# Group 1's attention steps on a three-slot pitch with early key and query transposes, and weight splits ordered behind activations

## The chip, the cores and the metric

One core of a Trainium2 chip runs the kernel. The metric is the device time of one execution in microseconds (us); lower is better. Engines: PE is TensorE (matmuls and transposes), PEld its weight loads, DVE is VectorE, ACT is ScalarE, POOL is GpSimd, SP is SyncE, which here only issues DMAs.

## The reference

Inputs: q, k, v of 4 batches, 8 heads, 768 positions, 64 channels; two weight matrices, `w_in` 512 x 2048 and `w_out` 2048 x 512. All arithmetic is fp32.

```
scores = q @ k^T / 8, kept where key < n_sink (4) or 0 <= query - key < window (128)
a      = softmax(scores)                  (kept ones alone)
x      = (a @ v) with heads joined        -> 3072 tokens x 512
h      = x @ w_in
g      = h * erf(softplus(h))
out    = g @ w_out
```

## The kernel before, in words

The 3072 tokens are cut into 12 groups of 256 tokens, three to a batch. A group has an attention part and an MLP part.

**Attention** of a group is 4 steps, one per pair of heads; `s` counts steps over the whole kernel, so group 0 has steps 0 to 3, group 1 steps 4 to 7, group 2 steps 8 to 11. A step is a chain across engines:

- `prep` (L274): PE transposes two blocks of keys and two of queries into the PSUM tile `tqk`, and ACT copies it into the tile `kq` (L284), which has one place per head pair, used again by every group.
- `core`, `score` (L289, L298): PE forms the scores `ps` (L329), DVE swaps triangles (`copy_predicated`, L341), adds the mask and takes the row extremum (L346), ACT takes the exponential (L350).
- `norm` (L354): DVE forms the reciprocal of the sum (L357, L358), DVE or, for steps 4 to 7, ACT scales the rows (L365 or L363), DVE makes the sink part (L369).
- `ptrans` (L374): PE transposes the probabilities (`tp`, L381) and the sink part (`ts`, L382), ACT copies them out (L385, L390), POOL cuts triangles with four selects (L395).
- `av` (L400): PE multiplies by the values (L422); `xfin` (L428): ACT and DVE write the result as a high and a low part, `xh` and `xl` (L440, L441); group 0 has one fp32 tile, `xf` (L435).
- `kcopy` (L260) keeps the last key block for the next group, by an ACT copy in group 0 and by a DMA from SP later; `next_dup` (L246) refills the tile `vz` with group 1's values by three DMAs from SP.

`tqk`, `tp`, `ts` and `av` are tiles of one PSUM pool, `ps_t`, with two buffers (L141), taken in turn in the order of the program; the scores have a single buffer, `ps_s`.

**MLP** of a group is 16 positions `f`. `hidden` (L601) multiplies by a 128-column block of `w_in`, `act` (L614) works once per two positions on a 128 x 512 tile: ACT runs a tanh and five squares (L622, L623, L624, three times L627), DVE three products (L631). `project` (L640) multiplies by a block of `w_out` and accumulates. Two PSUM buffers hold `h`, each for a pair of positions; one comes free for the pair after next with the first product of its `act`.

Weights arrive as 32 blocks of 512 KB. `wconv` (L501) converts each with three DVE instructions (L511, L516, L519) into the plain block `wf`. Group 0 multiplies plain blocks alone (L606 and L649). Later hidden products (L610) and, from group 2, projections (L652 to L654) use blocks split in a high and a low part: `wsplit` (L523) rounds on ACT (L527) and subtracts on DVE (L528).

**Order.** Program time is cut into slots `a`; the MLP position `m` (16 g + f) is emitted in slot `m + 10`, its projection four slots later. `plan` (L452) says which stage of which step is emitted in which slot: `core` of a step in slot `pos(s)`, the others relative to it. Every emitted instruction has a priority, `256 * slot` plus an offset by kind (`O`, L45: attention -400 to -50, `act` -400, `wconv` 0, `ws` (split) 300, projection 900). A scheduler walks a simulated timeline and gives each engine, whenever it is free there, the most urgent instruction that is ready. The resulting order of each engine's queue is fixed, and on the chip every queue runs in that order. `follow` (L265) adds an order between two instructions of one engine, without a wait.

For steps 4 to 7 the slots before are 5, 9, 13 and 17 (`4 * s - 11`), their `prep` one slot ahead of that, their `av` two steps later, in `core(s + 2)`: slots 13, 17, 21 and 25. `wsplit` of block n is emitted in the slot of `m = 11 + n` for `w_in`, and of `m = 24 + 1.5 (n - 16)` for `w_out`.

Of the kernel before, what the change touches and what calls it, by code (L numbers as in the profile page):

```python
# [9 lines left out]
F32 = mybir.dt.float32  # L10
# [3 lines left out]
AF = mybir.ActivationFunctionType  # L14
ALU = mybir.AluOpType
# [14 lines left out]
CC = (-0.3597576685435788, 7.2931830957863735, 0.5777779046187317)  # L30
CK = 0.018644221205607978
CS = CK ** (1 / 6)
# [7 lines left out]
NE, AL = 4, 2  # L40
# [12 lines left out]
def kernel(  # L53
# [11 lines left out]
    nc = tc.nc  # L65
# [3 lines left out]
    NPAIR = H // 2  # L69
# [8 lines left out]
    scale = 1.0 / math.sqrt(D)  # L78
# [8 lines left out]
    b_a = [CS * a for a in CA]  # L87
# [43 lines left out]
    def fast_path():  # L131
        with ExitStack() as st:
# [19 lines left out]
                out=kw[:, :256], in0=rf[:, :256], scalar=0.0, in1=kw[:, :256], op0=ALU.is_ge, op1=ALU.mult  # L152
# [136 lines left out]
            def core(s):  # L289

                prev = None
                late = s - AL >= NE
                if late:
                    prev = av(s - AL)
                if s < NSTEP:
                    score(s, prev)
# [103 lines left out]
            def av(s):  # L400

                g, c = divmod(s, NPAIR)
                d = stp[s]
                gb = g % GPB
                a = d["av"] = ps_t.tile([P, GT], F32, tag="t", name=f"av_{s}")
                vt, pz = d["v"], d["pz"]
                pa = d["pa"].rearrange("p h i t -> p h (i t)")
                ops = []
                for j, (t0, t1) in enumerate(((0, HP), (HP, 3 * HP), (3 * HP, GT))):
                    if j > 0 or gb > 0:  # L410
                        x = vt[j] if isinstance(vt, list) else vt[:, j]
                        ops.append((x, pa[:, :, t0:t1], t0))
                for i in range(2):
                    for z, hf in enumerate((lo, hi)):
                        ops.append((vz[:, z, i, 2 * c : 2 * c + 2], pz[:, :, i, hf], P * i + HP * z))
                prev = None
                for m, (x, y, t0) in enumerate(ops):
                    for h in range(2):
                        o = a[64 * h : 64 * h + 64, t0 : t0 + y.shape[-1]]
                        prev = follow(  # L420
                            prev,
                            nc.tensor.matmul(  # L422
                                o, x[:, h, :], y[:, h, :], start=(m == 0), stop=(m == len(ops) - 1), skip_group_check=True
                            ),
                        )
                return prev
# [16 lines left out]
            def at(a, what):  # L443

                key = int(a * PW) + O[what] + (E.get(what, 0) if a < EA else 0)
                return tc.high_priority(offset=tc.tile_snap_priority() + 1 - key)

            def pos(s):

                return s if s < NE else 4 * s - 11  # L450

            plan = {}  # L452
            for s in range(NSTEP + AL):
                if s < NSTEP:
                    for what, fn, a in (
                        ("prep", prep, pos(s) - (3 if s < NE or s >= 2 * NPAIR else 1)), ("norm", norm, pos(s) + 1), ("ptrans", ptrans, pos(s) + 2),
                        ("load", load, pos(s) - 4),
                    ):
                        if what == "load":
                            if s < 2 * NPAIR:  # L460
                                continue
                            plan.setdefault(a, []).append(("load", load_v, s))
                        plan.setdefault(max(a, 0 if what == "prep" else -1), []).append((what, fn, s))
                    if s >= 2 * NPAIR:
                        plan.setdefault(pos(s) - 2, []).append(("dup", dup, s))
                    if s // NPAIR % GPB < GPB - 1:
                        plan.setdefault(pos(s) + (2 if s < NE else 1), []).append(("kcopy", kcopy, s))
                plan.setdefault(pos(s), []).append(("core", core, s))
                if s < NE:
                    plan.setdefault(pos(s) + 3, []).append(("av", av, s))  # L470
                    plan.setdefault(pos(s) + 4, []).append(("xfin", xfin, s))
                elif s - AL >= NE:
                    plan.setdefault(pos(s) + 1, []).append(("xfin", xfin, s - AL))
            STAGES = ("av", "xfin", "norm", "ptrans", "kcopy", "prep", "core", "dup", "load")

# [44 lines left out]
                    out=ti, in0=w[:, :, 0], scalar=29, in1=ti, op0=ALU.logical_shift_right, op1=ALU.bitwise_or  # L520
                )

            def wsplit(n):  # L523

                t = wf[n]
                d = wt[n] = wpool.tile([P, 2, DM], F32R, tag="wo", name=f"wt_{n}")
                nc.scalar.copy(d[:, 0, :], t)  # L527
                nc.vector.tensor_tensor(d[:, 1, :], t, d[:, 0, :].bitcast(F32), op=ALU.subtract)  # L528

            def wblock(n):  # L530
                if n < 16:
# [4 lines left out]
            mlp = make_mlp(work, ps_h, ps_o)  # L536
# [15 lines left out]
            for m in range(-LEAD, NG * NF + LAG + 2):  # L552
                a = m + LEAD
                live = 0 <= m < NG * NF
                if live:
                    g, f = divmod(m, NF)
                    if f % 2 == 0:
                        hp = mlp.hid_tile(m)
                    if f > 0:
                        with at(a, "hid"):  # L560
                            mlp.hidden(hp, xp[g], f)
                attn(a)
                w = m - LAG
                if 0 <= w < NG * NF:
                    g2, f2 = divmod(w, NF)
                    with at(a, "proj"):
                        mlp.project(gs[w // 2], g2, f2)
                    if f2 == NF - 1:
                        for i in range(2):
                            r0 = (g2 * 2 + i) * P  # L570
                            with at(a, "res"):
                                nc.sync.dma_start(out[r0 : r0 + P, :], mlp.result(g2, i))
                if live:
                    if f == 0:
                        with at(a, "hid"):
                            mlp.hidden(hp, xp[g], f)
                    if f % 2 == 1:
                        with at(a, "act"):
                            gs[m // 2] = mlp.act(hp, m, g < 2)

                while wn < 32 and a >= 1 and (wn < (0, 1, 3, 5)[a - 1] if a < 5 else wn < 2 * a - 4 or need(order[wn]) <= m + W1):
                    with at(a, "wc"):
                        wconv(order[wn], wn)
                    wn += 1
                    with at(a, "wl"):
                        for n in order[wl : wn + WQ]:
                            wload(n)
                            wl += 1
                for n in split.get(m, ()):
                    with at(a, "ws"):  # L590
                        wsplit(n)

    class make_mlp:
        def __init__(self, work, ps_h, ps_o):
            self.work, self.ps_h, self.ps_o = work, ps_h, ps_o
            self.acc = {}

        def hid_tile(self, m):
            return self.ps_h.tile([P, 2, GT], F32, tag="h", name=f"h_{m}")
# [14 lines left out]
        def act(self, hp, m, whole=False):  # L614
            work = self.work
            h = hp.rearrange("p a t -> p (a t)")
            r = work.tile([P, 512], F32, tag="r", bufs=1, name=f"r_{m}")
            if whole:
                acc = work.tile([P, 2, 512], F32, tag="g", bufs=2, name=f"gf_{m}")[:, 0, :]
            else:  # L620
                acc = None
            nc.scalar.activation(r, h, AF.Tanh, bias=b_t, scale=0.5)  # L622
            nc.scalar.activation(r, r, AF.Square, bias=b_v, scale=-0.5)  # L623
            nc.scalar.activation(r, r, AF.Square, bias=b_r)  # L624
            for i in range(3):
                u = work.tile([P, 512], F32, tag="u", bufs=UB, name=f"u{i}_{m}")
                nc.scalar.activation(u, r, AF.Square, bias=b_a[i], scale=CS)  # L627
                x = h if i == 0 else acc
                if acc is None:
                    acc = u  # L630
                nc.vector.scalar_tensor_tensor(out=acc, in0=u, scalar=CC[i] * CS**2, in1=x, op0=ALU.add, op1=ALU.mult)  # L631
            if whole:
                return (acc,)
            gt = work.tile([P, 2, 512], F32R, tag="g", bufs=2, name=f"g_{m}")
            gh, gl = gt[:, 0, :], gt[:, 1, :]
            nc.vector.tensor_copy(gh, acc)  # L636
            nc.gpsimd.tensor_tensor(gl, acc, gh.bitcast(F32), op=ALU.subtract)  # L637
            return gh, gl
# [168 lines left out]
```

## Time and profile before

| | |
|---|---|
| median of 3 runs | 775.43 us (774.27 to 777.92) |
| the profiled execution | 773.4 us |
| its span, first to last instruction | 771.6 us |
| mean granted TensorE clock | 0.978 of full speed |
| busy share of the span: PE, PEld, DVE, ACT, POOL | 94%, 78%, 64%, 71%, 26% |

The profile cuts the span in 40 slices of 19.3 us, so one can see at what time an engine was busy, not only how much on average. Each wait is put down to the instruction that released it. PE's busy time is modelled, since matmuls overlap; the start-to-start distance of a run of equal matmuls is the better measure of their cost.

### The profile page before, as it was taken

What the parts mean: (1) busy time and instruction counts of PE and PEld (TensorE: products, weight loads), DVE (VectorE), ACT (ScalarE), POOL (GpSimd) and SP (SyncE); (2) the same over time, 40 slices, a digit from 0 to 9 for tenths busy, and PEclk for the clock granted to TensorE, in tenths of its full rate; (3) what the DMA queues carried; (4) which work ended last, traced back from release to release, by engine and by line L of the source; (5) the groups of instructions that cost most, each with busy time, mean ns of one, the idle gap of its engine ahead of it and who ended that gap; (6) DMA issues with size and microseconds to landing.
All of it is one profiled execution on the core that took longest, in us unless ns stands there. A gap on an engine that the chain in (4) does not pass through costs nothing. (4 is left out here: it accounts for less than half of the span.)

```text
span 771.6 us, 16346 instructions
## 1 busy us (share of the span) xinstructions
PE 728.0 (94%) x5808; PEld 603.5 (78%) x5808; DVE 496.0 (64%) x1375; ACT 549.2 (71%) x1293; POOL 202.4 (26%) x281
## 2 busy tenths in 40 slices
PE   6689946999999999999999999999999999999997
PEld 3456624776788888888888888888888888888895
DVE  7999983566477476476476476476476476576352
ACT  4476855887597588588598587587597597597572
POOL 1220102201233332232242242242242242242221
PEclk9899969999999999999999999999999999999999
DMA  9999002211122122122222222212212212210000
GB/s 196 257 330 364 15 0 45 66 39 34 41 69 52 49 57 56 48 51 51 55 51 61 53 51 59 51 47 55 55 48 61 55 49 57 52 34 1 29 1 32
DMA packets 115112, 53.59 MB, mean 69 GB/s; under 512 B 93840, under 2 KB 107664, under 8 KB 115024
## 3 DMA queue, kind: packets, MB, share of 16 engines
q1 hardware_dynamic: 114192, 52.33, 25.8%
q8 instruction: 49, 0.80, 0.4%
q14 instruction: 39, 0.32, 0.1%
q10 hardware_dynamic: 832, 0.13, 0.1%
HBM read 38.54 MB, written 6.29 MB: 58 GB/s over the span
## 5 line engine op out<-in xcount | busy, mean ns | idle before, releaser
L610 PE MATMUL h<-xh,wt 128*128 128x256 f32 x1408 | 273.0, 284 | 10.3 <-DVE gf L631 7.3
L610 PEld LDWEIGHTS h<-xh,wt 128*128 128x128 f32 x1408 | 223.3, 188 | 19.0 <-DVE gf L631 7.2
L610 PE MATMUL h<-xl,wt 128*128 128x256 f32 x704 | 198.3, 283 | 0.0
L627 ACT ACTIVATE u<-r 128x512 f32<-128x512 f32 x288 | 161.5, 622 | 9.9 <-DVE gf L631 2.2
L637 POOL TENSOR_TENSOR g<-u,g 128x512 fp32r<-128x512 f32 x80 | 104.1, 1302 | 241.7 <-DVE g L636 216.7
L610 PEld LDWEIGHTS h<-xl,wt 128*128 128x128 f32 x704 | 132.3, 188 | 4.8 <-issue 1.0
L395 POOL TENSOR_SCALAR_AFFINE_SELECT pz<-pa 64x256 f32<-64x256 f32 x96 | 52.1, 543 | 313.2 <-ACT pa L385 310.0
L652 PE MATMUL o<-wt,g 128*128 128x512 f32 x320 | 129.5, 405 | 0.1
L631 DVE SCALAR_TENSOR_TENSOR u<-u,u 128x512 f32<-128x512 f32 x160 | 119.0, 744 | 15.9 <-ACT u L627 1.0
L653 PE MATMUL o<-wt,g 128*128 128x512 f32 x320 | 127.9, 400 | 0.0
L654 PE MATMUL o<-wt,g 128*128 128x512 f32 x320 | 124.5, 399 | 0.3 <-POOL g L637 0.2
L631 DVE SCALAR_TENSOR_TENSOR u<-u,h 128x512 f32<-128x512 f32 x80 | 54.9, 686 | 81.0 <-ACT u L627 75.5
L350 ACT ACTIVATE pst<-pst,neg 128x144 f32<-128x144 f32 x192 | 77.6, 406 | 15.1 <-DVE neg L346 13.2
L622 ACT ACTIVATE r<-h 128x512 f32<-128x512 f32 x96 | 57.0, 594 | 41.5 <-PE h L610 34.1
L654 PEld LDWEIGHTS o<-wt,g 128*128 128x128 f32 x320 | 59.0, 188 | 12.7 <-POOL g L637 0.6
L653 PEld LDWEIGHTS o<-wt,g 128*128 128x128 f32 x320 | 60.2, 188 | 11.0
L652 PEld LDWEIGHTS o<-wt,g 128*128 128x128 f32 x320 | 60.2, 188 | 10.7 <-issue 0.3
L649 PE MATMUL o<-wf,gf 128*128 128x512 f32 x128 | 60.2, 613 | 3.2 <-DVE gf L631 3.2
L624 ACT ACTIVATE r<-r 128x512 f32<-128x512 f32 x96 | 60.7, 633 | 2.7
L623 ACT ACTIVATE r<-r 128x512 f32<-128x512 f32 x96 | 61.0, 635 | 2.0
L636 DVE CAST g<-u 128x512 fp32r<-128x512 f32 x80 | 36.4, 455 | 36.1 <-PE o L654 32.8
L441 DVE TENSOR_TENSOR xl<-av,xh 128x256 fp32r<-128x256 f32 x44 | 18.5, 420 | 55.5 <-ACT xh L440 54.9
(85 smaller groups left out, 968.3 us busy)
## 6 DMA issues: line engine op xcount, KB each, us to landing
ws<-in_moe_w_in_dram SPq DMA_DIRECT2D x16, 512.0 KB, 6.7
ws<-in_moe_w_out_dram SPq DMA_DIRECT2D x16, 512.0 KB, 9.0
out_dram<-ot SPq DMA_DIRECT2D x24, 256.0 KB, 2.2
v<-in_v_dram SPq DMA_DIRECT2D x56, 96.0 KB, 2.4
q<-in_q_dram SPq DMA_DIRECT2D x80, 64.0 KB, 2.1
k<-in_k_dram SPq DMA_DIRECT2D x80, 64.0 KB, 2.1
vz<-v SPq DMA_DIRECT2D x80, 64.0 KB, 2.1
kq<-kq SPq DMA_DIRECT2D x28, 64.0 KB, 1.9
```

The costliest lines, as they stand in the source:

```text
L350: nc.scalar.activation(y, y, AF.Exp, bias=d["neg"][:, i, h : h + 1], scale=-1.0, accum_out=d["sum"][:, i, h : h + 1])
L610: nc.tensor.matmul(o, wt[NC * j + c][:, p, fs], xt[e][:, c, :], start=(m == 0), stop=(m == len(ops) - 1))
L622: nc.scalar.activation(r, h, AF.Tanh, bias=b_t, scale=0.5)
L623: nc.scalar.activation(r, r, AF.Square, bias=b_v, scale=-0.5)
L624: nc.scalar.activation(r, r, AF.Square, bias=b_r)
L627: nc.scalar.activation(u, r, AF.Square, bias=b_a[i], scale=CS)
L631: nc.vector.scalar_tensor_tensor(out=acc, in0=u, scalar=CC[i] * CS**2, in1=x, op0=ALU.add, op1=ALU.mult)
L637: nc.gpsimd.tensor_tensor(gl, acc, gh.bitcast(F32), op=ALU.subtract)
L649: nc.tensor.matmul(o, gt[0][:, ws], wf[16 + f], start=(f == 0), stop=(f == NF - 1))
L652: nc.tensor.matmul(o, gh[:, ws], wt[16 + f][:, 0, :], start=(f == 0), stop=False)
L653: nc.tensor.matmul(o, gh[:, ws], wt[16 + f][:, 1, :], start=False, stop=False)
L654: nc.tensor.matmul(o, gl[:, ws], wt[16 + f][:, 0, :], start=False, stop=(f == NF - 1))
```

## The change

Three things. `pos(s)` of steps 4 to 7 becomes `3 * s - 6` (slots 6, 9, 12, 15), with `prep` in slots 4, 4, 5 and 6, and `av` and `xfin` three and four slots behind the step's own `core`, as group 0 has them. `av` inside a later `core` begins with step 8. And each split's ACT and DVE instruction is given an order (`follow`) behind the last square and the last product of the `act` of an earlier pair: a split emitted at position m stands behind the pair of number `(m - 1) // 2 - 1`.

```diff
-                late = s - AL >= NE
+                late = s - AL >= 2 * NPAIR
...
-                return s if s < NE else 4 * s - 11
+                return s if s < NE else 3 * s - 6 if s < 2 * NPAIR else 4 * s - 11
...
-                        ("prep", prep, pos(s) - (3 if s < NE or s >= 2 * NPAIR else 1)), ("norm", norm, pos(s) + 1), ("ptrans", ptrans, pos(s) + 2),
+                        ("prep", prep, max(4, s - 1) if NE <= s < 2 * NPAIR else pos(s) - 3), ("norm", norm, pos(s) + 1), ("ptrans", ptrans, pos(s) + 2),
...
-                if s < NE:
+                if s < 2 * NPAIR:
                     plan.setdefault(pos(s) + 3, []).append(("av", av, s))
                     plan.setdefault(pos(s) + 4, []).append(("xfin", xfin, s))
-                elif s - AL >= NE:
+                elif s - AL >= 2 * NPAIR:
                     plan.setdefault(pos(s) + 1, []).append(("xfin", xfin, s - AL))
...
-            def wsplit(n):
+            def wsplit(n, m):
...
-                nc.scalar.copy(d[:, 0, :], t)
-                nc.vector.tensor_tensor(d[:, 1, :], t, d[:, 0, :].bitcast(F32), op=ALU.subtract)
+                x, y = mlp.mark[(m - 1) // 2 - 1]
+                follow(x, nc.scalar.copy(d[:, 0, :], t))
+                follow(y, nc.vector.tensor_tensor(d[:, 1, :], t, d[:, 0, :].bitcast(F32), op=ALU.subtract))
...
-                        wsplit(n)
+                        wsplit(n, m)
...
-                nc.scalar.activation(u, r, AF.Square, bias=b_a[i], scale=CS)
+                sq = nc.scalar.activation(u, r, AF.Square, bias=b_a[i], scale=CS)
...
-                nc.vector.scalar_tensor_tensor(out=acc, in0=u, scalar=CC[i] * CS**2, in1=x, op0=ALU.add, op1=ALU.mult)
+                pr = nc.vector.scalar_tensor_tensor(out=acc, in0=u, scalar=CC[i] * CS**2, in1=x, op0=ALU.add, op1=ALU.mult)
+            if isinstance(m, int):
+                self.mark[m // 2] = sq, pr
```

## Rows read from the trace of the kernel before

**Rows 1.** The page: busy tenths of the 40 slices (19.3 us each), and the granted clock of PE in tenths.
```profile
PE   6689946999999999999999999999999999999997
DVE  7999983566477476476476476476476476576352
PEclk9899969999999999999999999999999999999999
```

**Rows 2.** Busy time of each engine in stretches of 10 us. Columns: stretch, its length, busy us (and instructions) of PE, PEld, DVE, ACT, POOL, then PE's granted clock, DMA share, GB/s.
```profile
20.00:30.00 10.00, 4.64 (x34) 3.48 (x33) 9.70 (x39) 4.93 (x21) 1.87 (x4) 0.74 0.92 227
30.00:40.00 10.00, 7.44 (x81) 5.32 (x81) 9.53 (x18) 3.89 (x9) 4.95 (x8) 0.92 0.95 304
40.00:50.00 10.00, 7.63 (x51) 6.20 (x52) 9.91 (x29) 7.92 (x23) 0.00 (x0) 0.93 1.04 306
...
90.00:100.00 10.00, 7.37 (x34) 3.28 (x32) 10.00 (x19) 9.23 (x18) 0.00 (x0) 0.99 0.03 9
100.00:110.00 10.00, 2.13 (x5) 1.32 (x6) 9.91 (x18) 3.70 (x6) 0.00 (x0) 0.50 0.00 0
110.00:120.00 10.00, 9.44 (x25) 4.27 (x23) 2.87 (x14) 4.36 (x16) 0.00 (x0) 0.83 0.00 0
120.00:130.00 10.00, 6.61 (x88) 5.27 (x87) 4.51 (x16) 6.56 (x20) 3.48 (x7) 0.86 0.21 48
130.00:140.00 10.00, 6.76 (x78) 4.84 (x75) 5.55 (x21) 5.39 (x16) 2.56 (x6) 0.84 0.18 40
140.00:150.00 10.00, 9.38 (x105) 8.58 (x102) 6.39 (x23) 8.71 (x23) 2.06 (x4) 0.96 0.22 48
150.00:160.00 10.00, 10.00 (x55) 7.01 (x54) 7.21 (x23) 9.84 (x23) 0.00 (x0) 1.00 0.34 95
```

**Rows 3.** PE's timeline, 60 to 139 us: start, length, instruction, count, and in brackets the idle time before it and its releaser. L281 is `prep`, L329 the scores, L381 the transposes of the probabilities, L422 `av`.
```profile
60.81 0.99 PE L329 MATMUL ps<-kq 64*64 64x208 f32 x16
...
85.20 0.38 PE L281 MATMUL tqk<-ident,k_early 128*128 128x128 f32 x2
...
93.88 0.99 PE L329 MATMUL ps<-kq 64*64 64x208 f32 x16
...
104.68 0.58 PE L610 MATMUL h<-xh,wt 128*128 128x256 f32 x1 [6.38 <-DVE gf L631]
...
108.88 9.41 PE L649 MATMUL o<-wf,gf 128*128 128x512 f32 x16 [3.20 <-DVE gf L631]
...
119.40 0.44 PE L281 MATMUL tqk<-ident,k_early 128*128 128x128 f32 x2 [0.56 <-ACT pz L390]
...
121.17 0.99 PE L329 MATMUL ps<-kq 64*64 64x208 f32 x16
...
126.59 0.33 PE L381 MATMUL tp<-ident,pst 128*128 128x128 f32 x1 [3.15 <-ACT pst L363]
...
135.18 0.89 PE L381 MATMUL tp<-ident,pst 128*128 128x128 f32 x4 [2.62 <-DVE pst L365]
...
136.89 0.72 PE L422 MATMUL av<-pa,v_early 128*64 128x64 f32 x12 [0.62 <-ACT pa L385]
137.37 1.10 PE L422 MATMUL av<-pz,vz 128*64 128x64 f32 x16
```

**Rows 4.** ACT's timeline, 88 to 104 us, same columns; L527 is the split's rounding, L627 the last instructions of an `act`.
```profile
88.01 5.84 ACT L527 CAST wt<-wf 128x512 fp32r<-128x512 f32 x11
...
104.06 0.63 ACT L627 ACTIVATE u<-r 128x512 f32<-128x512 f32 x1
```

**Rows 5.** Groups of DVE's instructions from 88 to 112.3 us: line, operation, count | busy us, mean ns | idle before.
```profile
L528 DVE TENSOR_TENSOR wt<-wf,wt 128x512 fp32r<-128x512 f32 x21 | 13.5, 687 | 0.0
```

**Rows 6.** DVE's timeline, 96 to 126 us: the first product of positions 12 and 13 (it alone reads `h`), the first of step 6's four masks, the last product of group 0, then what a step costs DVE (here `xl` of step 5, and swaps and sink part of step 7).
```profile
96.86 0.70 DVE L631 SCALAR_TENSOR_TENSOR gf<-u,h 128x512 f32<-128x512 f32 x1
...
110.66 0.31 DVE L346 CUSTOM_DVE_ANT_0 pst<-ps,mask 128x144 f32<-128x144 f32 x1
...
111.58 0.69 DVE L631 SCALAR_TENSOR_TENSOR gf<-u,gf 128x512 f32<-128x512 f32 x1
...
122.20 0.41 DVE L441 TENSOR_TENSOR xl<-av,xh 128x256 fp32r<-128x256 f32 x1
122.64 0.90 DVE L341 COPY_PREDICATED ps<-tri,ps 64x256 f32<-64x256 int8 x2
...
126.08 0.29 DVE L369 TENSOR_TENSOR snk<-pst,sum 128x128 f32<-128x128 f32 x1
```

**Rows 7.** Groups of PE's instructions from 48 to 97 us, same columns as Rows 5.
```profile
L649 PE MATMUL o<-wf,gf 128*128 128x512 f32 x48 | 21.9, 594 | 0.0
```

**Rows 8.** POOL's timeline: the triangle selects of step 4 and of step 6, first pair of each.
```profile
54.73 3.73 POOL L395 TENSOR_SCALAR_AFFINE_SELECT pz<-pa 64x256 f32<-64x256 f32 x2 [14.86 <-ACT pa L385]
...
120.02 0.90 POOL L395 TENSOR_SCALAR_AFFINE_SELECT pz<-pa 64x256 f32<-64x256 f32 x2 [34.95 <-ACT pa L385]
```

**Rows 9.** DMA issues: line by tile, engine, count, KB each, median us from issue to landing.
```profile
vz<-v SPq DMA_DIRECT2D x80, 64.0 KB, 2.1
...
vz<-v_early SPq DMA_DIRECT2D x2, 128.0 KB, 10.2
```

**Rows 10.** SP's timeline of DMA issues: start, time from the first to the last of them, line, count. The last of the three `next_dup` issues, and the key copy of step 6.
```profile
53.76 0.46 SPq L250 DMA_DIRECT2D vz<-v_early  x1
...
94.56 0.50 SPq L129 DMA_DIRECT2D kq<-kq  x1
```

**Rows 11.** Waits of PE after 150 us: who waited for whom, total us, times, longest.
```profile
PE h L610 <- DVE u L631: 3.0, 8, 0.4
```

More of the change, by code (lines that the diff above doesn't have):

```diff
@@ L595, in __init__ @@
             self.work, self.ps_h, self.ps_o = work, ps_h, ps_o
-            self.acc = {}
+            self.acc, self.mark = {}, {}
         def hid_tile(self, m):
```

## The prediction, as it stood before the run

> **What bounds the kernel now.** I read the forty slices first, then stretches of 10 us where they dip, then the timelines of PE, ACT and DVE there. PE is at 9 tenths in nearly every slice from 140 us on [rows 1], so PE is the bound and a gain must be a hole in its line. There are two: the start, up to 50 us, and 90 to 150 us. In the second, PE is busy 7.37, 2.13, 9.44, 6.61, 6.76 and 9.38 of each 10 us [rows 2]: 41.7 of 60, so 18.3 us idle. From 150 us PE is full again, so what is closed there comes off the end.
>
> Two things make the hole. First, splits: ACT rounds eleven weight blocks from 88.0 to 93.9 us, and the `act` of positions 14 and 15 ends only with the square at 104.06 [rows 4]. DVE does 21 splits in 13.5 us between 88 and 112.3 [rows 5]; the first product of the pair before stands at 96.86, the last of group 0 at 111.58 [rows 6]. PE waits 6.38 and 3.20 us for such products [rows 3]. Secondly, attention: scores of steps 5, 6 and 7 come at 60.81, 93.88 and 121.17, the last two 8.7 and 1.8 us behind their own `prep` (85.20, 119.40), and the last `av` that group 1's hidden products need ends at 138.5; meanwhile PE waits 3.15 and 2.62 us for a step's scaled rows [rows 3]. A `prep` comes late because its PSUM tile is taken in turn behind `tp` and `ts` of the step before.
>
> **What may come back.** The idle time, 18.3 us. Then the clock: it is 0.50 in 100 to 110 us, where PE worked 2.13 us, and 0.83 to 0.96 until 150 [rows 2]. Group 0's last sixteen projections took 9.41 us [rows 3]; at the pace before they would take 16 x 21.9/48 = 7.3 [rows 7], so 2.1 us. For PE's other 22.8 busy us of 120 to 150, a clock near 0.85 against 1.00 bounds the loss at 22.8 x 0.15 = 3.4, and 0 bounds it below. I take 2.9, since the projections, the nearest row, did run slower in full: 5.0 in all (bounds 2.1 and 5.5). Together 23.3 us.
>
> **Does the work fit ahead of it?** DVE is full from 20 to 110 us [rows 1, 2], so its sum decides. A split at position m is ordered behind the `act` two or three positions earlier, which lets only six blocks (m = 11 to 16) go ahead of group 0's last `act`; 15 of the 21 leave, 15 x 13.5/21 = 9.6 us. What comes in is step 7 (swaps 0.90, four masks at 0.31, sink part 0.29, all shown, and about 0.3 for the reciprocal: 2.7 us) and three `xl` of 0.41: 3.9 us [rows 6]. Group 0's last product moves from 112.3 to about 106.6. PE: its projections end at 118.3; without the waits of 6.38 and 3.20 and the 2.1 us of clock, at 106.6. Three `av` (1.58 each, from 136.89 to 138.47), two sets of transposes (1.1), scores (0.99) and `prep` (0.88) of the steps moved ahead put back 8.8, at durations of the low clock [rows 3]: PE is done with all of it by 115, behind DVE. So PE can be full, and group 1's hidden products then need nothing more.
>
> **What the change costs.**
> - Four `prep` behind group 0's: three come earlier than before, as three more tiles in the turn of the two-buffer pool ahead of group 0's last `av`. Bounds: 4.3 us lost, three times a `prep` and the wait of 0.56 before one [rows 3]; 2.4 gained, if its products (0.8) only fill idle time. Between 20 and 50 us PE has 10.3 us idle and ACT more [rows 2], which covers them. I take 1.0 lost, nearer the cover.
> - 15 splits move behind 112 us, beside the 11 of the 32 that ran there. ACT has little room at first, 9.84 of 10 us at 150 [rows 2]. Queued behind a split on ACT stands the next square, for which DVE's product, then PE's hidden product wait. Bounds: 0, and 15 x 5.84/11 = 8.0 us [rows 4]. Those 11 and all later work left PE a wait of 3.0 us in all, at most 0.4 at a time [rows 11], so I take 2.0. The order itself adds no wait.
> - `av` of step 4 follows `next_dup` by one slot, not five. Its three DMAs were issued until 53.76 [rows 10] and took 10.2 us, where later ones take 2.1 [rows 9]: `vz` is there at 64. The first two of the step's four selects end at 58.5 [rows 8]. PE stops in its queue for 0 to 5.5 us, and everything behind it, hidden products included, waits. I take 1.0, since the rest of the selects and a queue of products stand between.
> - SP: key copies of steps 6 and 7 move from slots 14 and 18 to 13 and 16, and may stand ahead of the last weight loads, where step 6's copy came at 94.56 [rows 10]. A copy waits in SP's queue for its step's scores, the loads behind it too. The DMA share is down to 0.03 by 90 us [rows 2], so they have room; 0 to 5 us, I take 0.
> - POOL: the selects of the moved steps run beside a full DVE. A pair took 3.73 us at 54.73 and 0.90 at 120.02 [rows 8]: 2.8 us a pair, latency on a chain with three slots for a step. 0 to 3 us; I take 0.
> - Holes left by handing over between queues whose order was made on a simulated line: 0 to 6.4, the longest wait there [rows 3]; I take 1.5, as DVE's sum ends 8 us ahead of PE's.
>
> Sum: 23.3 - 1.0 - 2.0 - 1.0 - 1.5 = 17.8. The profiled execution, 773.4 us (span 771.6 and 1.8 around it), becomes 755.6; the median of the runs stands 2.0 higher, so **757.6 us**.
>
> The selects' rows show POOL losing beside a full DVE. The Trainium skill (SBUF — State Buffer, Who interferes with whom) says more: GpSimd and a DVE instruction with two SBUF inputs, or in a two-port mode, exclude each other through a shared port, and whichever issues first makes the other wait for its whole length. By that rule DVE may pay too, and the sum would go as in rival 3.
>
> **Rivals.**
> 1. *Steps keep their pace.* The late `prep` was not the brake; the hand-overs in DVE's full queue are. Step 6's scores came at 93.88 [rows 3], its first mask at 110.66 [rows 6]: 17 us of a pitch of 27 to 33. With 2 to 9 us saved a step (`prep` to scores), the last `av` ends some 10 us earlier, near 128, and the 23.3 become 10 less costs of 1 to 2: 767 for the runs. Against: scores of a step no longer stand behind transposes of the last, and three slots of priority replace four.
> 2. *Slower: splits in the way of `act`.* The place is `h`'s buffer: a hidden pair waits for the first product of the pair two before. If each of the 26 held-back splits comes ahead of that product, it adds 0.53 us of ACT and 0.64 of DVE [rows 4, 5]: 26 x 1.17 = 30.4, so 773.4 - 23.3 + 30.4 = 780.5, some 782.5 for the runs. It decides once ACT's queue for a pair is longer than PE's. For it: the 0.4 us waits at this very place [rows 11], and ACT's 9.84. Against: they are only 3.0 us in 620.
> 3. *POOL and DVE block each other.* Sixteen selects of 0.45 us, each holding DVE for its length, cost 7.2 us: group 0's last product at 113.8, its last eight projections (3.6 us) behind it at 117.4, and with hand-overs 4 to 5 us of the gain are lost: 762. Against: in the rows that show it, POOL waits, and nothing shows DVE waiting.
> 4. *Not what it says.* The slots are priorities alone. Step 5 was planned for slot 9 before too, ahead of the MLP's first position, and its scores ran at 60.81 [rows 3]. If the scheduler again places steps by readiness and moves the hole elsewhere, the time is 775.
>
> **How the numbers follow.** About 0.5% (3.9 us) is what a measurement of this kernel can tell from no change: 771.6 to 779.3. Forecast 0.60, rival 1 0.14, rival 3 0.06: faster 0.80. Rival 4: same 0.09. Rival 2: slower 0.11. The range: all of the clock, preps that fill idle time and no other cost give 18.3 + 5.5 + 2.4 = 26.2, so 749.2 for the runs; at the other end it takes in rivals 1 and 3 and stops at 770, below rivals 4 and 2, which are 0.20.
>
> **What would show it.** Right: PE has under 6 us idle between 90 and 150 us of the new profile and its clock stays near 1.00; group 0's sixteen last projections run at 0.46 us each; the last `av` of group 1 ends before 115 us; ACT has no run of splits ahead of an `act`; splits spread from about 90 to 220 us. Costs: PE's idle time in 20 to 50 us grows over 10.3 by no more than 1 or 2; PE's wait for L631 after 110 us stays under 5. Wrong: scores of steps 5 to 7 still 27 us or more apart (rival 1), L610 waiting over 20 us for L631 (rival 2), DVE instructions stretched beside L395 (rival 3), an idle stretch elsewhere as long as the old one (rival 4).

## The result and the profile after

The changed kernel takes 754.14 us (median of 4 runs, 753.5 to 756.13) against 776.67 in the same job: a ratio of 0.9716, 95% interval 0.9679 to 0.9752. Timed once more, in another job, it took 755.21 us, 0.9737 (0.9716 to 0.9759). The forecast was 757.6 us. The profiled execution has a span of 751.5 us, 20.1 less than before. Lines from 527 on are one to three higher than before: L527 is now L528, L606 L607, L610 L611, L624 L625, L631 L632, L649 L652.

The page after, the same lines as [rows 1]:

```profile
PE   6779899999999999999999999999999999999997
DVE  7999996665786665665665675576476476386342
PEclk9699999999999999999999999999999999999999
```

The dip of PE at 100 to 135 us is gone, and there is one digit of 8 where 9 stood, at 75 to 94 us. Stretches of the changed kernel, columns as in [rows 2]:

```profile
0.00:50.00 50.00, 33.98 (x281) 23.72 (x281) 43.46 (x162) 25.70 (x83) 10.79 (x25) 0.86 0.95 249
50.00:90.00 40.00, 35.40 (x216) 23.04 (x218) 39.03 (x96) 30.79 (x79) 18.11 (x12) 1.00 0.74 253
90.00:150.00 60.00, 59.81 (x390) 41.86 (x387) 44.35 (x109) 47.69 (x108) 7.62 (x15) 1.00 0.15 36
150.00:200.00 50.00, 48.30 (x398) 35.60 (x397) 31.32 (x96) 36.61 (x95) 9.10 (x16) 1.00 0.25 60
200.00:751.50 551.50, 542.78 (x4534) 475.39 (x4532) 336.96 (x918) 405.28 (x932) 166.40 (x215) 1.00 0.19 47
```

The same stretches of the kernel before:

```profile
0.00:50.00 50.00, 33.68 (x255) 22.59 (x256) 43.72 (x157) 26.12 (x84) 10.33 (x25) 0.92 0.96 247
50.00:90.00 40.00, 40.00 (x187) 27.57 (x187) 39.61 (x82) 28.19 (x58) 8.03 (x8) 0.97 0.69 249
90.00:150.00 60.00, 41.67 (x325) 27.56 (x324) 39.24 (x108) 37.94 (x98) 8.10 (x16) 0.83 0.11 24
150.00:200.00 50.00, 50.00 (x359) 35.05 (x360) 29.02 (x81) 38.36 (x89) 6.43 (x12) 1.00 0.18 44
200.00:771.60 571.60, 562.61 (x4695) 490.76 (x4686) 344.46 (x952) 418.56 (x967) 169.46 (x220) 1.00 0.20 48
```

Length less PE's busy time gives its idle time: 16.3, 0, 18.3, 0 and 9.0 us before, 16.0, 4.6, 0.2, 1.7 and 8.7 after. The hole of 18.3 us closed to 0.2; 4.6 opened at 50 to 90 us and 1.7 at 150 to 200. In sum 43.6 became 31.2, so 12.4 of the 20.1 us are idle time. The other 7.7 are PE's busy time, 728.0 to 720.3 for the same 5808 matmuls. The clock of 90 to 150 us rose from 0.83 to 1.00 and that of 50 to 90 from 0.97, while that of 0 to 50 fell from 0.92 to 0.86. These are the stretches from 48 us on in which the kernel before had a clock of 0.50, columns as above; the changed kernel stands at 1.00 in every stretch from 50 us on:

```profile
48.60:52.10 3.50, 3.50 (x10) 2.79 (x9) 3.50 (x8) 3.40 (x8) 0.00 (x0) 0.51 0.92 306
99.80:113.50 13.70, 5.63 (x9) 2.75 (x10) 12.98 (x31) 5.67 (x15) 0.00 (x0) 0.50 0.00 0
127.10:130.60 3.50, 3.29 (x39) 2.62 (x42) 0.03 (x1) 1.90 (x6) 1.67 (x4) 0.51 0.02 5
137.40:140.80 3.40, 3.40 (x42) 2.46 (x38) 2.39 (x5) 1.51 (x3) 1.51 (x3) 0.50 0.01 2
```

PE is busy for 15.8 us in them. Sixteen scores take 1.77 us there (at 138.40) and 0.99 at full clock (at 121.17), so, as an estimate, about half of the 15.8 was lost to the clock, near the 7.7. At the start the two kernels are even: PE is busy for 33.7 us of the first 50 before and for 34.0 after.

PE's timeline after, as [rows 3]:

```profile
42.34 0.44 PE L281 MATMUL tqk<-ident,k_early 128*128 128x128 f32 x2
...
42.93 0.99 PE L329 MATMUL ps<-kq 64*64 64x208 f32 x16
...
50.45 0.99 PE L329 MATMUL ps<-kq 64*64 64x208 f32 x16 [1.30 <-DVE neg L346]
...
56.48 0.34 PE L422 MATMUL av<-pa,v_early 128*64 128x64 f32 x4 [0.85 <-POOL pa L395]
57.23 0.55 PE L422 MATMUL av<-pa,v_early 128*64 128x128 f32 x8 [0.41 <-POOL pa L395]
...
61.45 0.99 PE L329 MATMUL ps<-kq 64*64 64x208 f32 x16
...
84.77 0.34 PE L422 MATMUL av<-pa,v_early 128*64 128x64 f32 x4 [1.94 <-POOL pa L395]
85.59 0.55 PE L422 MATMUL av<-pa,v_early 128*64 128x128 f32 x8 [0.48 <-POOL pa L395]
...
102.16 0.69 PE L422 MATMUL av<-pz,vz 128*64 128x64 f32 x16
...
103.26 3.60 PE L652 MATMUL o<-wf,gf 128*128 128x512 f32 x8
106.30 0.68 PE L611 MATMUL h<-xh,wt 128*128 128x256 f32 x1
...
115.73 3.70 PE L652 MATMUL o<-wf,gf 128*128 128x512 f32 x8
...
120.67 1.88 PE L652 MATMUL o<-wf,gf 128*128 128x512 f32 x4
```

All four transposes of group 1 are over by 43 us; scores of steps 5 to 7 come at 42.93, 50.45 and 61.45, where they came at 60.81, 93.88 and 121.17; the last `av` ends at 102.85, not 138.5, and group 1's hidden products begin at 106.30, ahead of group 0's last sixteen projections, which stand between 113.86 and 122.55. ACT's splits now stand in small lots between the squares, as in these lines of ACT's timeline (compare [rows 4]):

```profile
95.69 2.17 ACT L528 CAST wt<-wf 128x512 fp32r<-128x512 f32 x4
97.76 0.63 ACT L625 ACTIVATE r<-r 128x512 f32<-128x512 f32 x1
...
100.62 1.12 ACT L528 CAST wt<-wf 128x512 fp32r<-128x512 f32 x2
...
106.40 1.13 ACT L528 CAST wt<-wf 128x512 fp32r<-128x512 f32 x2
```

And POOL's selects of steps 4 to 6, with the first DVE lines behind the long one (POOL's timeline, then DVE's):

```profile
52.54 3.41 POOL L395 TENSOR_SCALAR_AFFINE_SELECT pz<-pa 64x256 f32<-64x256 f32 x2 [11.20 <-ACT pa L385]
...
63.66 2.59 POOL L395 TENSOR_SCALAR_AFFINE_SELECT pz<-pa 64x256 f32<-64x256 f32 x2 [6.49 <-ACT pa L385]
...
76.15 8.09 POOL L395 TENSOR_SCALAR_AFFINE_SELECT pz<-pa 64x256 f32<-64x256 f32 x2 [7.81 <-ACT pa L385]
84.30 1.23 POOL L395 TENSOR_SCALAR_AFFINE_SELECT pa<-pa 64x256 f32<-64x256 f32 x2
```

```profile
83.87 0.69 DVE L632 SCALAR_TENSOR_TENSOR gf<-u,h 128x512 f32<-128x512 f32 x1
84.46 0.80 DVE L519 SCALAR_TENSOR_TENSOR wf<-ws,wf 128x512 int32<-128x512 int32 x1
85.18 0.64 DVE L511 TENSOR_SCALAR wf<-ws 128x512 int32<-128x512 int32 x1
```

A pair of selects that takes 0.90 us where DVE is idle as it starts [rows 8] took 8.09. The pair ends as DVE works on a product that reads `h` from PSUM (83.87), and only then do DVE's next instructions stretch, 0.80 for 0.70 and 0.64 for 0.43.

### The profile page after: what moved, and what is told of

The parts are those of the page before. It is cut to its first block, busy times and chain, and to the rows that moved or that the text cites. A ratio compares the mean times of both kernels' runs of the same rounds, so it can differ in the third digit from the quotient of the medians.

```text
span 751.5 us, 16337 instructions
## 1 busy us (share of the span) xinstructions
PE 720.3 (96%) x5808; PEld 599.6 (80%) x5808; DVE 495.1 (66%) x1375; ACT 546.1 (73%) x1293; POOL 212.0 (28%) x281
## 5 line engine op out<-in xcount | busy, mean ns | idle before, releaser
L611 PE MATMUL h<-xh,wt 128*128 128x256 f32 x1408 | 271.4, 284 | 3.7 <-DVE u L632 3.5
L611 PEld LDWEIGHTS h<-xh,wt 128*128 128x128 f32 x1408 | 222.7, 188 | 12.9 <-DVE u L632 5.8
L611 PE MATMUL h<-xl,wt 128*128 128x256 f32 x704 | 199.0, 283 | 0.0
L395 POOL TENSOR_SCALAR_AFFINE_SELECT pz<-pa 64x256 f32<-64x256 f32 x96 | 61.4, 640 | 291.0 <-ACT pa L385 287.9
L611 PEld LDWEIGHTS h<-xl,wt 128*128 128x128 f32 x704 | 132.3, 188 | 5.2 <-issue 1.8
L632 DVE SCALAR_TENSOR_TENSOR u<-u,u 128x512 f32<-128x512 f32 x160 | 117.4, 734 | 15.5
L632 DVE SCALAR_TENSOR_TENSOR u<-u,h 128x512 f32<-128x512 f32 x80 | 54.8, 685 | 80.4 <-ACT u L628 79.9
L657 PEld LDWEIGHTS o<-wt,g 128*128 128x128 f32 x320 | 59.3, 188 | 12.4 <-POOLq L778 0.5
L625 ACT ACTIVATE r<-r 128x512 f32<-128x512 f32 x96 | 60.7, 632 | 2.8
L624 ACT ACTIVATE r<-r 128x512 f32<-128x512 f32 x96 | 60.9, 634 | 1.8
L652 PE MATMUL o<-wf,gf 128*128 128x512 f32 x128 | 59.0, 596 | 0.0
```

Of the source, the lines that this page charges most:

```text
L395: nc.gpsimd.affine_select(out=out, in_=x, pattern=[[0, 2], [0, 2], [-sg, HP]], compare_op=op, fill=0.0, base=0, channel_multiplier=sg,)
L611: nc.tensor.matmul(o, wt[NC * j + c][:, p, fs], xt[e][:, c, :], start=(m == 0), stop=(m == len(ops) - 1))
L632: pr = nc.vector.scalar_tensor_tensor(out=acc, in0=u, scalar=CC[i] * CS**2, in1=x, op0=ALU.add, op1=ALU.mult)
L652: nc.tensor.matmul(o, gt[0][:, ws], wf[16 + f], start=(f == 0), stop=(f == NF - 1))
L657: nc.tensor.matmul(o, gl[:, ws], wt[16 + f][:, 0, :], start=False, stop=(f == NF - 1))
```

## The experiments

My reading was that the two causes add up, and that within the second it is the late `prep` that holds a step back. Ratios are to the kernel before, timed in the same job, with 95% intervals.

**The two parts, each alone.** Steps moved, splits as before:

```diff
-                follow(x, nc.scalar.copy(d[:, 0, :], t))
-                follow(y, nc.vector.tensor_tensor(d[:, 1, :], t, d[:, 0, :].bitcast(F32), op=ALU.subtract))
+                nc.scalar.copy(d[:, 0, :], t)
+                nc.vector.tensor_tensor(d[:, 1, :], t, d[:, 0, :].bitcast(F32), op=ALU.subtract)
```

> The steps moved as in the change, splits without their order. Two causes in series (my reading): group 1's attention is done by about 105 us, but runs of splits again stand ahead of group 0's last activations, so PE waits some 6 to 9 us for L632 near 95 to 110 us; 760 to 765 us. Attention alone made the hole: 753 to 756 us. Splits alone made it: 772 to 777 us.

762.85 us, 0.983 (0.9779 to 0.9881). The last `av` ends at 109, but ACT rounds seven and six blocks in a row again, and PE waits for the products and for two selects. PE's waits from 84 to 130 us:

```profile
PE h L611 <- DVE gf L632: 3.9, 2, 2.1
PE av L422 <- POOL pa L395: 2.9, 2, 2.6
```

Splits ordered, steps as before (the change with `pos`, `prep`, `av` and `late` of the kernel before):

> Splits ordered as in the change, the steps as before. Two causes in series: group 0's projections end near 106 us, then PE idles while steps 6 and 7 still come 27 us apart; 765 to 772 us. Splits alone made the hole: 753 to 757 us. Attention alone made it: 774 to 777 us.

764.61 us, 0.9863 (0.9817 to 0.9909), 0.4 us under the range of my reading. Group 0's projections end at 108, but scores of steps 6 and 7 still come at 93.52 and 111.03 and the last `av` ends at 128. PE's longest waits from 90 to 140 us are the step's chain, as before, and one for a product:

```profile
PE tp L381 <- ACT pst L363: 2.7, 1, 2.7
PE tp L381 <- DVE pst L365: 2.6, 1, 2.6
PE o L652 <- DVE gf L632: 2.2, 1, 2.2
```

Against 774.66 in that job the parts alone win 11.8 and 10.1 us, 21.9 in sum; both together win 20.0 to 22.5 in their two jobs. So they add, and neither hides the other.

**What in the moved steps does it.** First the change with late transposes:

```diff
-                        ("prep", prep, max(4, s - 1) if NE <= s < 2 * NPAIR else pos(s) - 3), ("norm", norm, pos(s) + 1), ("ptrans", ptrans, pos(s) + 2),
+                        ("prep", prep, pos(s) - (3 if s < NE or s >= 2 * NPAIR else 1)), ("norm", norm, pos(s) + 1), ("ptrans", ptrans, pos(s) + 2),
```

> The change with the key and query transposes of steps 4 to 7 back one slot ahead of their step. If the late prep was the brake: scores of steps 5 to 7 fall back to 17 us or more apart (8 to 11 us in the changed kernel), the last av ends 10 us later or more, 757 to 764 us. If the slots alone matter: 753 to 756 us.

771.56 us, 0.9964 (0.9939 to 0.9989): worse than the range of my reading, and 7 us worse than not moving the steps at all. Scores come at 42.85, 70.02, 105.81 and 118.22. Then the reverse, early transposes with the old slots and the old, late `av`:

```diff
-                return s if s < NE else 3 * s - 6 if s < 2 * NPAIR else 4 * s - 11
+                return s if s < NE else 4 * s - 11
...
-                late = s - AL >= 2 * NPAIR
+                late = s - AL >= NE
...
-                if s < 2 * NPAIR:
+                if s < NE:
...
-                elif s - AL >= 2 * NPAIR:
+                elif s - AL >= NE:
```

> The change with steps 4 to 7 back in slots 5, 9, 13, 17 and their av two steps later, the early transposes kept. If the late prep was the brake: most of the gain of moving the steps stays, 754 to 762 us. If the slots and the earlier av matter: as with the split order alone, 765 to 772 us.

763.47 us, 0.9854 (0.9781 to 0.9928), no better than the splits alone. Scores of steps 5 to 7 do come earlier, at 50.55, 75.50 and 98.03, but `av` still waits for the step two behind, and the last one ends at 128.8. The expectations took one as the brake and the other as free; both are needed. Last, early transposes and early `av`, with the old pitch of four slots:

```diff
-                return s if s < NE else 3 * s - 6 if s < 2 * NPAIR else 4 * s - 11
+                return s if s < NE else 4 * s - 11
```

> The change with steps 4 to 7 back on four slots (5, 9, 13, 17), early transposes and av three slots behind each step kept. If early transposes and early av carry the gain: the last av ends by 110 us and the time is 753 to 757 us. If the three-slot pitch is needed: scores stay 22 to 25 us apart as in the run with early transposes and old slots, the last av ends past 115 us, 758 to 764 us.

753.6 us, 0.9722 (0.9677 to 0.9768), the whole gain. (This kernel leaves out a wait: its `av` of step 4 comes ahead of `next_dup` and reads group 0's part of `vz`. In the change PE does not wait for `vz`, so the times can be compared.) Scores come at 46.36, 52.82 and 63.10, as early as with three slots: the slots are priorities, and once the inputs are ready the steps run ahead of either pitch. The pitch does nothing that shows in the time.

**Why a late transpose holds a step.** The late-transpose kernel, with `tqk` of steps 4 to 7 in the scores' buffer:

```diff
-                tp = ps_t.tile([P, 4, P], F32, tag="t", name=f"tqk_{s}")
+                if NE <= s < 2 * NPAIR:
+                    tp = ps_s.tile([P, 2, 512], F32, tag="s", name=f"tqk_{s}")[:, 0, :].rearrange("p (n t) -> p n t", n=4)
+                else:
+                    tp = ps_t.tile([P, 4, P], F32, tag="t", name=f"tqk_{s}")
```

> The run with late transposes once more, but the keys and queries of steps 4 to 7 are transposed into the buffer of the scores, not into one of the two buffers that tp, ts and av take in turn. If the turn of the two buffers made a late transpose a brake: scores of steps 5 to 7 come 8 to 20 us apart instead of 27, 36 and 12, the last av ends before 115 us, 753 to 760 us. If the late place in the plan is the brake whatever the buffer: 768 to 774 us.

762.02 us, 0.9829 (0.9803 to 0.9854): between the two ranges. Out of the turn, scores come at 47.72, 65.88 and 89.10 and 9.5 of the 16 to 17 us that the late transposes cost are back. So the turn of the two buffers is the larger part of it; the transposes now need the scores' one buffer instead, and what that costs is not measured. Of the rest, PE waits 4.37 us for one step's selects here:

```profile
96.04 0.48 PE L425 MATMUL av<-pa,v_early 128*64 128x64 f32 x4 [4.03 <-POOL pa L398]
96.86 0.91 PE L425 MATMUL av<-pa,v_early 128*64 128x128 f32 x8 [0.34 <-POOL pa L398]
```

**Which half of the split's order counts.** The order on ACT alone (the second `follow` taken away):

> The change with the order of the splits on ACT alone; DVE's half is free to stand anywhere behind its ACT half. If the harm was ACT's run of roundings ahead of the squares: as the change, 752 to 757 us. If DVE's subtractions ahead of the products were the harm: the wait for products comes back in part, 757 to 763 us.

756.02 us, 0.9745 (0.9698 to 0.9792), as the change: ACT's runs of roundings were the harm, and DVE's halves, which need them, follow.

**The new hole at 50 to 90 us.** DVE's conversions replaced by copies with one input, which leave out the lower words of the weights:

```diff
-                first = nc.vector.tensor_scalar(
-                    ti, w[:, :, 1], 0x07FFFFFF, 3, op0=ALU.bitwise_and, op1=ALU.logical_shift_left
-                )
+                def single(n):
+                    return nc.vector.tensor_reduce(
+                        t[:, :n], w[:, :n, 1:2].bitcast(F32), axis=AX.X, op=ALU.max
+                    )
+
+                first = single(256)
...
-                nc.vector.scalar_tensor_tensor(
-                    out=ti, in0=w[:, :, 1], scalar=-0x40000000, in1=ti, op0=ALU.bitwise_and, op1=ALU.bitwise_or
-                )
-                mark["c", wn] = nc.vector.scalar_tensor_tensor(
-                    out=ti, in0=w[:, :, 0], scalar=29, in1=ti, op0=ALU.logical_shift_right, op1=ALU.bitwise_or
-                )
+                single(512)
+                mark["c", wn] = single(512)
```

> The change with the three conversion instructions of a weight block replaced by copies with a single SBUF input of about the same length (0.3, 0.6, 0.6 us), so that the weights hold their upper words only; DVE stays as full as it was. If POOL's selects wait for DVE instructions that read two SBUF inputs or run in a two-port mode: the pairs of selects of steps 4 to 7, 3.41, 2.59, 8.09 and 1.33 us in the changed kernel, fall to 1 to 2 us, PE's waits for them (0.85, 0.41, 1.94, 0.48 us) mostly go, and the time falls by 2 to 5 us, to 749 to 752. If a full DVE as such, or the order of the queues, delays them: selects and time as in the changed kernel, 753 to 756 us.

749.54 us, 0.967 (0.9628 to 0.9711). The selects, beside a DVE that is busy 9.87 to 10.00 of every 10 us from 50 to 100:

```profile
51.87 1.19 POOL L395 TENSOR_SCALAR_AFFINE_SELECT pz<-pa 64x256 f32<-64x256 f32 x2 [12.41 <-ACT pa L385]
...
61.59 0.91 POOL L395 TENSOR_SCALAR_AFFINE_SELECT pz<-pa 64x256 f32<-64x256 f32 x2 [7.04 <-ACT pa L385]
...
73.52 1.47 POOL L395 TENSOR_SCALAR_AFFINE_SELECT pz<-pa 64x256 f32<-64x256 f32 x2 [9.39 <-ACT pa L385]
```

3.41, 2.59 and 8.09 us became 1.19, 0.91 and 1.47, and PE's waits for them went. So it is not a full DVE but the kind of its instructions that keeps the selects out. L516 and L519 read two SBUF inputs; L511 reads one; which of them does it is not told apart by this run. The Trainium skill (SBUF — State Buffer, Who interferes with whom) has a GpSimd instruction that reads SBUF wait for a VectorE instruction with two SBUF inputs or in a two-port mode, and for that instruction's length. The trace agrees with the first part, not with the second: the pair of 8.09 us lasted over a dozen DVE instructions. By their ratios this run is some 4 to 5 us faster than the change, and PE's idle time at 50 to 90 us is 0.5 us, where the change has 4.6. The copies are a little shorter, 0.594 us in the mean against 0.614, which the run does not separate from the selects.

`av` of steps 4 to 7 two slots later:

```diff
+                    x = 3 if s < NE else 5
-                    plan.setdefault(pos(s) + 3, []).append(("av", av, s))
-                    plan.setdefault(pos(s) + 4, []).append(("xfin", xfin, s))
+                    plan.setdefault(pos(s) + x, []).append(("av", av, s))
+                    plan.setdefault(pos(s) + x + 1, []).append(("xfin", xfin, s))
```

> The change with av and xfin of steps 4 to 7 two slots later. If PE's waits for the selects near 56 and 85 us are only a matter of where av stands in PE's queue: PE has other work ahead, idle time in 50 to 90 us falls from 4.6 to under 2 us, 750 to 753 us. If the later av only passes the wait on (two PSUM buffers taken in turn hold back the next step's transposes): 753 to 760 us.

757.79 us, 0.9765 (0.9707 to 0.9823), no better than the change: the wait is passed on. PE still stops 1.95 and 0.48 us for step 6's selects, now at 87.9 us. And the selects of steps 4 to 7 on DVE, as products with a 0/1 tile (`mz`, made once at the start):

```diff
...
+                        if NE <= s < 2 * NPAIR:
+                            y = mz[hf, 0 if out is not x else 1].rearrange("p (a b t) -> p a b t", a=1, b=1)
+                            nc.vector.tensor_tensor(out, x, y.broadcast_to([HP, 2, 2, HP]), op=ALU.mult)
+                            continue
                         nc.gpsimd.affine_select(
```

> The change with the triangles of steps 4 to 7 cut by DVE, as products with a 0/1 tile, and no longer by POOL's selects. PE's waits for the selects (0.85, 0.41, 1.94, 0.48 us) go, and so do the DVE instructions that a select holds; DVE gets 16 products of about 0.33 us, 5.3 us, on its full stretch. If PE's idle time there is what counts: 750 to 753 us. If DVE's sum sets group 0's last products: 754 to 759 us.

758.1 us, 0.9795 (0.9767 to 0.9822), beside 755.21 for the change:

> The changed kernel again, on the same chip as the run with selects on DVE: 752 to 757 us.

PE's idle time at 50 to 90 us falls from 4.6 to 2.1 us, but the time does not follow. DVE's products do pay: PE now waits for products of `act` there (1.2 and 1.0 us). And at 150 to 200 us PE is idle for 4.7 us, against 1.7, mostly in the chain of a later group's step, and its clock falls there:

```profile
170.00:180.00 10.00, 7.67 (x71) 4.84 (x69) 2.78 (x14) 3.97 (x14) 1.66 (x4) 1.00 0.15 34
180.00:190.00 10.00, 9.13 (x78) 7.79 (x79) 4.09 (x21) 4.52 (x16) 1.66 (x4) 0.66 0.24 52
```

Why the queues came out so there is open. No version that computes the same beat the change.

## Why the prediction was right

- **The hole and what closes it: right.** 18.3 us of idle time at 90 to 150 us [rows 2] became 0.2, and the two parts of the change, run alone, show both causes at work.
- **The clock: under-sized.** I took 5.0 us (bounds 2.1 and 5.5); busy time fell by 7.7. Group 0's last sixteen projections take 7.6 us, in four lots (forecast 7.3), and the clock is 1.00 from 40 us on. The bound was drawn for 97 to 150 us alone, and too low there: of the 15.8 us that PE was busy at a clock of 0.50, 12.3 lie there, and half of that is 6.2. The other 3.5, at 48.6 to 52.1, I had not counted.
- **DVE's sum: right that the work fits, late in its times.** Six splits stand ahead of group 0's last product, as forecast, but it ends at 109.26 (forecast 106.6): its pair's first product waited 1.12 us for PE's projections. Group 1's last `av` ends at 102.85, but group 0's last projections at 122.55 (forecast for both: by 115). That cost nothing, because PE was filled with group 1's hidden products meanwhile. In DVE's timeline:

```profile
106.97 0.69 DVE L632 SCALAR_TENSOR_TENSOR gf<-u,h 128x512 f32<-128x512 f32 x1 [1.12 <-PE o L652]
107.77 1.49 DVE L632 SCALAR_TENSOR_TENSOR gf<-u,gf 128x512 f32<-128x512 f32 x2
```

- **Early `prep`, 1.0 us of cost: none that shows, within its bounds.** PE's idle time at 20 to 50 us fell from 10.3 to 8.2, at a lower clock (0.77 against 0.86); at 0 to 20 it rose by 1.8, so the start is even in sum.
- **Splits, 2.0 us: at most that.** After 105 us PE waits 3.5 us at `h`'s buffer (3.0 before), 0.2 for a product of `act` in group 1, and 1.3 for an ACT copy of a step at 180 to 190; whether the last is the splits' doing is not shown.
- **`next_dup`, 1.0 us: nothing.** `av` of step 4 waited for selects, not for `vz`. The key copies cost nothing that shows.
- **POOL, 0 us: wrong.** It is the cost that failed. I put the slow selects down as latency with room, in three slots; PE's queue has none once `av` is its next instruction. PE's waits for them at 45 to 95 us are 3.7 us, above my bound of 3:

```profile
PE av L422 <- POOL pa L395: 3.7, 4, 1.9
PE ps L329 <- DVE neg L346: 1.3, 1, 1.3
PE h L607 <- DVE gf L632: 0.5, 1, 0.5
```

- **Hand-overs, 1.5 us:** the other two lines above, 1.8 us.

So costs of 5.5 us were forecast and 5.9 came (18.3 of idle time less 12.4 net), of another make; that the sums agree is luck. Of the 3.5 us between 757.6 and 754.1, 2.7 are PE's busy time (7.7 for 5.0); most of the rest is that the median stands 0.6 above the profiled execution (753.5) where I had added 2.0.

Of the rivals, steps that keep their pace and a hole that only moves elsewhere did not come, though the premise of the latter, that slots are priorities alone, held for the pitch. Splits in the way of `act` did not either: PE's waits at `h`'s buffer stayed as small as in [rows 11]. POOL and DVE blocking each other did come, but with POOL as the one that loses most, and at 3.7 us of PE's time. That nothing showed DVE waiting was misread: in the trace of before an L519 at 33.32 us, beside two selects, took 0.90 us, where the one at 31.95 took 0.69. What I had not put right is the reason for the steps' gain: I gave it to early transposes and to three slots for four. The slots are nothing, and early transposes are worth nothing without the early `av`.

## What to carry to other kernels

Where a pool of two buffers is taken in turn, a stage that needs its turn behind the slow stages of the step before can set the pace of the whole chain; look at the order of takers before the slots or priorities. Hold filler work (here the splits) behind the urgent work of the same queue by an order, since a list scheduler fills every gap that it believes in. And count a slow engine's latency as lost time wherever its result is the next thing in the bounding engine's queue.

## What was not expected of the hardware

A select takes some 0.45 us (half of a pair's 0.90), and DVE can shut it out for 6 us and more. The second select of the pair of 8.09 us in the changed kernel:

```profile
77.88 6.36 POOL L395 TENSOR_SCALAR_AFFINE_SELECT pz<-pa 64x256 f32<-64x256 f32 x1
```

Three L511 (at 78.44, 81.39 and 82.33) stand in these 6.36 us, and none let it in.

Whether selects are shut out goes with pauses in DVE's queue, some far shorter than a select. In the profiled execution of the change, DVE waited 0.56 us for a weight load at 32.6 us and the first pair of selects there took 1.29. In the profiled execution of the second timing, of the same program, DVE's queue has no such gap, and POOL's line reads:

```profile
32.24 5.92 POOL L395 TENSOR_SCALAR_AFFINE_SELECT pz<-pa 64x256 f32<-64x256 f32 x2 [7.62 <-ACT pa L385]
```

The run with the order on ACT alone has no gap there either, and its pair took 5.89. In the other eight runs that keep these conversions and in which the pair starts at 32 us, DVE's queue pauses, and the pair takes 1.27 to 2.38. The pause can be under 0.1 us: in the run with the steps alone the next conversion starts 0.65 us behind the last, where 0.60 is the distance without a pause.

What it does to the time is less clear. `av` of group 0 waits 4.71 us for the selects in the second timing's profiled execution, which took 760.65 us where the other five took 753.62 to 755.96. So a DMA that comes a little later may make the kernel faster. But the run with the order on ACT alone has the same wait, 4.7 us, in an execution of 757.05 us, and its other three took 754.65 to 758.76; so this is not shown.
